# Two bursts of key-value matmuls become one behind the first denominators, and all W' units move among the queries of blocks 2 and 3

## The chip, the core and the metric

The kernel runs on one NeuronCore of one Trainium2 chip. Its engines are TensorE (PE in the profile; its weight loads are PEld), VectorE (DVE), ScalarE (ACT), GpSimd (POOL) and SyncE (SP), which here issues nearly all DMA transfers. The time is the device time of one execution in microseconds; a comparison uses the median of several executions.

## The reference

Two branches A and B of linear attention read the same x (2048 tokens, 640 features, 32 heads of 20), each with its own weights, and are mixed by a gate per token:

```
q, k, v  = x @ wqkv                       # per branch
pq, pk   = phi(q), phi(k)                 # phi(t) = where(t > 0, t + 1, exp(t)) + 1e-6
kv[h]    = pk[h]^T @ v[h]                 # 20 x 20 per head
z[h]     = sum over tokens of pk[h]
o        = (pq @ kv) / (pq . z + 1e-6)    # per head
branch   = o @ wo
out      = g * branch_A + (1 - g) * branch_B,   g = sigmoid(sum(x * gate_w))
```

## The kernel before, in words

The kernel never forms v or o. With G = pk^T x (640 by 640 per branch) the key-value product of a head is a small block of G Wv, and kv and wo are folded into one matrix W', 640 by 640 per branch: row (h, d) of W' is kv[h][d, :] times the 20 rows of wo of head h. Then branch = (pq / den) @ W'. The stages, in the order of TensorE:

1. Keys (`k_part`, `k_both`): k = x Wk by token tiles of 128; ScalarE takes the exponential, VectorE forms phi.
2. G (`g_unit`, five units per branch, k = 0 to 4): 32 matmuls of 320 columns accumulate over the 16 token tiles; ScalarE copies the result to GS, a transposing DMA puts it into GT.
3. M (`m_unit`): the blocks of kv. 55 matmuls per branch, each with 64 stationary columns in one of two column halves of the array (g = 0 or 1) and 60 or 40 moving columns, all into one PSUM bank. Units q = 0 to 4 hold six heads (120 features) each, three in each half; q = 5 holds the last two heads and uses only one half, half 0 for A and half 1 for B. VectorE then multiplies by a constant mask (L647: two instructions of 60 x 300, one of 40 x 40) and writes MB, which has six slots that A and B use in turn; slot 5 is shared, A in its upper rows and B in its lower ones.
4. W' (`wp_unit`): per unit two matmuls of 320 columns (weights MB, moving operand the rows of wo) into a pair of PSUM banks, and one eviction to WS, by VectorE for three units of A (L680), by ScalarE for the rest (L682). There are 11 units: five per branch and one joint unit for slot 5. `wp_store` writes the 600 rows to DRAM, `wp_rows` the last 40, and reads all of it back in the row order of the queries, into WPA and WPB.
5. Queries (`q_unit`): blocks b = 0 to 3 of 512 tokens, two branches, k = 0 to 4: 40 units of five matmuls of 512 columns. ScalarE takes the exponential (L743) into one of six EK slots, VectorE does min and add (L747), then max and add (L752), which releases the unit's PSUM bank.
6. Denominators (`dens`), for blocks 0 and 1 together and for blocks 2 and 3 together: 20 matmuls of 512 columns with 32 stationary columns, four of them side by side, into one bank.
7. `scale_q` per block: ScalarE adds epsilon (L787), VectorE takes the reciprocal (L793), two DMAs spread the factor over the partitions, VectorE multiplies the queries (L811).
8. Final tiles (`final`): per token tile an A half and a B half of ten matmuls, ScalarE scales A by g (L859), VectorE adds B (L865), SP stores. At most three A halves can wait for their B halves (three TS slots).

**What sets the order.** The calls at the end of the function only list operations; each gets the next priority number. `_Sched.schedule` then plans: again and again it takes the operation that can start earliest, and among those of one engine within 20 ns of the earliest the one with the lowest number (L188). It books durations by formulas (`_act_ns`, `_dve_ns`: elements / 0.96 + 68 ns for a VectorE instruction at rate 1, so 0.38 us for a mask of 300) and 180 ns between an operation and one that needs its result. The eight PSUM banks are given out in the same walk (`place`, L157 to 165): a tile of two banks takes the aligned pair that was free first, a tile of one bank the bank that was free first, or one whose pair neighbour is busy among those within 300 ns. A bank is taken again when, by the book, its last reader has ended; on the chip the new user waits on that reader's semaphore. What results is one fixed list per engine, run in that order. Reciprocals and multiplies of `scale_q` may so run earlier than their place in the list of calls.

Before, the calls stand like this: M_A between the G units of B; A's W' units between the rest; M_B behind the queries of block 0; the joint unit and B's W' units among the queries of block 1, each two queries behind (WPLAG = 2); `scale_q(0)` ahead of the queries of block 2.

Of the kernel before, what the change touches and what calls it, by code (L numbers as in the profile page):

```python
# [15 lines left out]
ACT = mybir.ActivationFunctionType  # L16
# [3 lines left out]
D = 640  # L20
H = 32
DH = 20
NT = 16
NB = 4
NC = 5
EPS = 1e-6
HALF = 320
WPLAG = 2
XW = 672
PE_GHZ = 2.4  # L30

# [255 lines left out]
def _act_ns(n, psum=True):  # L287
    return n / 1.2 + (52.0 if psum else 94.0)


def _dve_ns(n, rate=1):
    return n / (0.96 * rate) + 68.0
# [6 lines left out]
def bass_gated_mix__linear_attn_block__linear_attn_block__prompt_kernel(nc, A_x, A_wqkv, A_wo, B_x, B_wqkv, B_wo, gate_w, out):  # L299
# [6 lines left out]
    with ExitStack() as es:  # L306
        E = es.enter_context

        def sb(name, shape, dtype=dt.bfloat16):
            return E(nc.sbuf_tensor(name, shape, dtype))  # L310
# [11 lines left out]
        PQ = {X: FE[:, x, :].rearrange("p (k s) -> p k s", s=S) for x, X in enumerate(XS)}  # L322
        WP = {X: sb("WP" + X, [128, NC, D]) for X in XS}
        W5 = sb("W5", [128, D])
        MB = sb("MB", [128, 6, 120])
        WS = sb("WS", [120, 6, D])
        WD = {X: nc.dram_tensor("wrows" + X, [D, D], dt.bfloat16) for X in XS}
        GS = sb("GS", [128, NC, D])
# [48 lines left out]
        def mms(name, steps, reads, writes, cols, lat=190.0, par=1, prio=None, after=None):  # L377


            def fn(pe):  # L380
                ins = None
                for o, l, r, a, z, tp in steps():
                    ins = pe.matmul(o, l, r, start=a, stop=z, tile_position=tp, skip_group_check=True)  # L383
                return ins

            return sch.op("PE", fn, cols / PE_GHZ / par, reads=reads, writes=writes, name=name, lat=lat, prio=prio, after=after)
# [17 lines left out]
        for X in XS:  # L404
            sch.op("POOL", lambda e, X=X: e.memset(WO[X][:, :, :], 0.0), 3000, writes=[("WO", X, 0), ("WO", X, 1)], name="woz" + X)
        sch.op("POOL", lambda e: e.memset(W5[:, :], 0.0), 500, writes=[("W5", X) for X in XS], name="w5z")
        sch.op("POOL", lambda e: e.memset(MB[:, :, :], 0.0), 700, writes=[("M", q) for q in range(6)], name="mz")
        def load_x(eng, t):
            dma(eng, "xn%d" % t, XN[:, t, 0:D], xin[128 * t : 128 * t + 128, :], writes=[("XN", t)], us=0.25)

# [201 lines left out]
        def zbd(X):  # L612
            sch.op(
                "DVE",
                lambda e: e.tensor_tensor(
                    out=ZBD[X][:, :, :], in0=CB[:, C_MH : C_MH + H].unsqueeze(1).to_broadcast([128, NC, H]),
                    in1=Z32[X][:, :].unsqueeze(2).to_broadcast([128, NC, H]), op=ALU.mult,
                ),
                _dve_ns(NC * H), reads=[("Z", X, k) for k in range(NC)] + [("CB",)], writes=[("ZBD", X)], name="zbd" + X,
            )  # L620

        def m_unit(X):

            tile = _Tile(1)
            last = XS.index(X)

            def steps():
                r = []
                for q in range(6):
                    w = 12 if q < 5 else 8  # L630
                    for j in range(NC):
                        for g in (0, 1) if q < 5 else (last,):
                            at = D * j + 120 * q + 60 * g * (q < 5)
                            r.append((
                                PS[64 * g : 64 * g + 64, tile.banks[0], 60 * q : 60 * q + NC * w], WV[X][:, at : at + 64],
                                GT[X][:, j, :, 24 * q + 12 * g * (q < 5) : 24 * q + 12 * g * (q < 5) + w], j == 0, j == NC - 1, (0, 64 * g),
                            ))
                return r

            mms("m%s" % X, steps, [("GT", X, k) for k in range(NC)] + [("WV", X), ("WVP", X)], [(tile,)], 25 * 75 + 400)  # L640
            for q0, q1, g, w in ((0, 5, 0, 12), (0, 5, 1, 12), (5, 6, last, 8)):
                n = DH * (w // 4)

                def mask(e, q0=q0, q1=q1, g=g, w=w, n=n):
                    p0 = 64 * g
                    m = CB[p0 : p0 + n, C_MM : C_MM + 60].rearrange("p (k i) -> p k i", i=12)[:, :, 0:w]
                    return e.tensor_tensor(  # L647
                        out=MB[p0 : p0 + n, q0:q1, 60 * g : 60 * g + n].rearrange("p q (i k) -> p q k i", k=NC),
                        in0=PS[p0 : p0 + n, tile.banks[0], 60 * q0 : 60 * q0 + n * (q1 - q0)].rearrange("p (q k i) -> p q k i", k=NC, i=w),
                        in1=m.unsqueeze(1).to_broadcast([n, q1 - q0, NC, w]), op=ALU.mult,  # L650
                    )

                sch.op(
                    "DVE", mask, _dve_ns(n * (q1 - q0)), reads=[(tile,), ("CB",)], writes=[("M", q) for q in range(q0, q1)],
                    name="mm%s" % X,
                )

        def wp_unit(X, q):

            tile = _Tile(2)  # L660
            w = W5 if q == 5 else WO[X][:, q, :]

            def steps():
                return [
                    (PS[0:120, tile.banks[h], 0:HALF], MB[0:124, q, :], w[0:124, HALF * h : HALF * h + HALF], True, True, None)
                    for h in (0, 1)
                ]

            mms(
                "wp%s%d" % (X, q), steps, [("M", q)] + [("W5", Y) for Y in XS if q == 5] + [("WO", X, g) for g in (0, 1) if q < 5],  # L670
                [(tile,)], D + 60,
            )
            dst = WS[:, q, :].rearrange("p (h f) -> p h f", f=HALF)

            def src():
                return PS[0:120, tile.banks[0] : tile.banks[1] + 1, 0:HALF]

            name = "wpe%s%d" % (X, q)
            if X == "A" and q % 2 == 0:
                sch.op("DVE", lambda e: e.tensor_copy(dst, src()), _dve_ns(D), reads=[(tile,)], writes=[("WS", q)], name=name)  # L680
            else:
                sch.op("ACT", lambda e: e.activation(dst, src(), ACT.Copy), _act_ns(D), reads=[(tile,)], writes=[("WS", q)], name=name)  # L682

        def wp_store(X):
            dma(
                "SP", "ws" + X, WD[X].ap()[0:600, :].rearrange("(q p) f -> p q f", p=120), WS[:, 0:5, :], reads=[("WS", q) for q in range(5)],
                writes=[("WD", X, 0)], us=2.0,
            )

        def wp_rows(X):  # L690

            nat = WD[X].ap()
            p0 = 60 * XS.index(X)
            dma("SP", "ws5" + X, nat[600:D, :], WS[p0 : p0 + 40, 5, :], reads=[("WS", 5)], writes=[("WD", X, 5)], us=0.2)
            dma(
                "SP", "wp" + X, WP[X][:, :, :], nat.rearrange("(i k) f -> i k f", k=NC), reads=[("WD", X, 0), ("WD", X, 5)],
                writes=[("WP", X, k) for k in range(NC)], us=2.2,
            )
# [59 lines left out]
        def dens(b0):  # L758

            dtile = _Tile(1)  # L760

            def den():
                r = []
                for k in range(NC):
                    for x, X in enumerate(XS):
                        q = PQ[X][:, k, 512 * b0 : 512 * b0 + 1024].rearrange("p (b h f) -> p b h f", b=2, h=2)
                        for h in (0, 1):
                            g = 2 * x + h
                            r.append((
                                PS[32 * g : 32 * g + 32, dtile.banks[0], :].rearrange("p (b f) -> p b f", b=2), ZBD[X][:, k, :],  # L770
                                q[:, :, h, :], k == 0, k == NC - 1, (0, 32 * g),
                            ))
                return r

            mms(
                "den%d" % b0, den, [("ZBD", X) for X in XS] + [("PQ", X, k, b) for X in XS for k in range(NC) for b in (b0, b0 + 1)],
                [(dtile,)], 5 * 540,
            )
            return dtile

        def scale_q(b, dtile, pieces):

# [116 lines left out]
            g_unit("A", k)  # L899
        zbd("A")  # L900
        gates()
        g_unit("B", 0)
        g_unit("B", 1)
        m_unit("A")
        g_unit("B", 2)
        for q in (0, 1):
            wp_unit("A", q)
        g_unit("B", 3)
        for q in (2, 3):
            wp_unit("A", q)  # L910
        g_unit("B", 4)
        wp_unit("A", 4)
        wp_store("A")
        zbd("B")
        def queries(b):
            for X in XS:
                for k in range(NC):
                    q_unit(X, b, k)
                    q = 5 * (X == "B") + k - WPLAG
                    if b == 1 and 0 <= q < 6:  # L920
                        wp_unit("B", (q - 1) % 6)
                        if q == 0:
                            wp_rows("A")

        def finals(b):
            for t in range(4 * b, 4 * b + 4):
# [3 lines left out]
                    final(t, ((0, 320), (320, 480), (480, D)), {320: 0, D: 320})  # L930

        queries(0)
        m_unit("B")
        queries(1)
        wp_store("B")
        wp_rows("B")
        d01 = dens(0)
        scale_q(0, d01, 2)
        queries(2)
        queries(3)  # L940
        scale_q(1, d01, 2)
        d23 = dens(2)
        finals(0)
        scale_q(2, d23, 2)
        finals(1)
# [36 lines left out]
```

## Time and profile before

| | us |
|---|---|
| median of 3 executions (190.44 to 191.15) | 190.88 |
| the profiled execution | 190.88 |
| its span, first to last instruction | 189.5 |
| TensorE busy | 185.9 |
| VectorE busy | 129.8 |
| ScalarE busy | 76.5 |
| M_A, M_B: start to the next matmul | 1.06 each |
| one query unit on TensorE | 1.08 |
| first denominators, start to the next matmul | 1.19 |
| last query matmul issued, first final tile | 142.31 |
| store of B's 600 rows, reload of WPB: issue to landing | 4.9, 4.5 |

In the lines of groups, "busy us, mean ns of one, idle time just before them" stand behind the bars. In the timeline, the first two columns are start and length; the length of a merged line runs to the end of its last instruction, and matmuls overlap, so the spacing of starts tells what a stretch costs. A release named behind an arrow is the instruction that ended a wait.

### The profile page before, as it was taken

Reading aid. Unit: us, or ns where it says so; the run is one execution under the profiler, and the core shown is the slowest. Engines: PE = TensorE matmul, PEld = TensorE weight load, DVE = VectorE, ACT = ScalarE, POOL = GpSimd, SP = SyncE. Lnnn points to the kernel's source line nnn. Section 1 sums busy time; section 2 is a strip of 40 time slices with the busy share of each in tenths; the row PEclk is TensorE's granted clock in tenths of the full one; section 3 lists DMA queues with packets and bytes.
Section 4 is the critical chain, followed back from the end, with each engine's and each line's share of the span. In section 5 each row is a group of like instructions: output and inputs, shape, how many; then the busy total and the mean of one; then the engine's idle time right before and its main releaser. Section 6 shows DMA issues by size and latency. Waiting matters only on the chain.

```text
span 189.5 us, 3208 instructions
## 1 busy us (share of the span) xinstructions
PE 185.9 (98%) x1289; PEld 124.0 (65%) x1289; DVE 129.8 (68%) x275; ACT 76.5 (40%) x129; POOL 8.2 (4%) x14
## 2 busy tenths in 40 slices
PE   7999999999999999999999999999999999999995
PEld 2555555555788888888855666455556677777774
DVE  1398998999600009996179997898999959933324
ACT  2265656565311122103255478565553422332232
POOL 8900000000000000000000000000000000000000
DMA  5999699991011111112143004675000173221212
GB/s 189 298 243 177 211 388 364 337 231 33 0 35 38 35 35 38 35 35 38 35 95 102 5 22 173 166 224 170 0 0 3 44 226 92 86 89 35 73 69 69
DMA packets 31936, 21.49 MB, mean 113 GB/s; under 512 B 16818, under 2 KB 31666, under 8 KB 31922
## 3 DMA queue, kind: packets, MB, share of 16 engines
q1 hardware_dynamic: 31490, 20.80, 39.5%
q10 hardware_dynamic: 432, 0.49, 0.8%
q8 instruction: 10, 0.16, 0.4%
q14 instruction: 4, 0.03, 0.1%
HBM read 12.05 MB, written 5.31 MB: 92 GB/s over the span
## 4 chain that ended last, share of the span: by engine, by line
PE 94%; DMA 3%; SPq 1%; issue 0%; ACT 0%; DVE 0%; DVEq 0%; ACTq 0%
PE ps L383 94%; DMA WK<-in_B_wqkv_dram 3%; SPq L372 1%; ACT TS L859 0%; DVE OL L865 0%; DVEq L276 0%; ACTq L276 0%
## 5 line engine op out<-in xcount | busy, mean ns | idle before, releaser
L383 PE MATMUL ps<-WK,XT 128*128 128x512 bf16 (+2 forms) x250 | 44.0, 337 | 0.5 <-DMA WK<-in_A_wqkv_dram 0.2
L383 PE MATMUL ps<-XN,FE 128*128 128x320 bf16 x320 | 44.3, 300 | 0.0
L383 PEld LDWEIGHTS ps<-XN,FE 128*128 128x128 bf16 x320 | 37.5, 118 | 5.9
L383 PEld LDWEIGHTS ps<-WK,XT 128*128 128x128 bf16 x250 | 24.1, 98 | 20.0 <-DMA WK<-in_A_wqkv_dram 0.5
L743 ACT ACTIVATE EK<-ps 128x512 bf16<-128x512 f32 x40 | 23.9, 597 | 18.5 <-PE ps L383 16.9
L563 ACT ACTIVATE EK<-ps 128x512 bf16<-128x512 f32 (+1 forms) x42 | 21.4, 526 | 16.2 <-PE ps L383 16.2
L752 DVE SCALAR_TENSOR_TENSOR FE<-ps,EK 128x512 bf16<-128x512 f32 x40 | 26.8, 688 | 0.7
L859 ACT ACTIVATE TS<-ps,GA 128x640 f32<-128x640 f32 (+2 forms) x18 | 13.2, 734 | 29.5 <-PE ps L383 29.5
L383 PE MATMUL ps<-WPB,FE 128*128 128x320 bf16 (+1 forms) x165 | 24.7, 295 | 0.0
L383 PE MATMUL ps<-WPA,FE 128*128 128x320 bf16 (+1 forms) x165 | 24.7, 295 | 0.0
L573 DVE SCALAR_TENSOR_TENSOR FE<-ps,EK 128x512 bf16<-128x512 f32 (+1 forms) x42 | 23.9, 596 | 0.5
L865 DVE SCALAR_TENSOR_TENSOR OS<-ps,GA,TS 128x640 bf16<-128x640 f32 x15 | 13.0, 869 | 14.7 <-PE ps L383 14.7
L383 PE MATMUL ps<-XT,WQA 128*128 128x512 bf16 x100 | 22.8, 380 | 0.0
L383 PE MATMUL ps<-XT,WQB 128*128 128x512 bf16 x100 | 22.7, 379 | 0.0
L600 ACT ACTIVATE GS<-ps 128x640 bf16<-128x640 f32 x10 | 7.0, 704 | 37.0 <-PE ps L383 37.0
L383 PEld LDWEIGHTS ps<-WPA,FE 128*128 128x128 bf16 x165 | 15.9, 98 | 6.1
L383 PEld LDWEIGHTS ps<-WPB,FE 128*128 128x128 bf16 x165 | 15.8, 98 | 6.2 <-ACT TS L859 0.4
L383 PEld LDWEIGHTS ps<-XT,WQB 128*128 128x128 bf16 x100 | 11.7, 117 | 9.1
L383 PEld LDWEIGHTS ps<-XT,WQA 128*128 128x128 bf16 x100 | 11.6, 118 | 9.4 <-issue 0.4
L705 DVE SCALAR_TENSOR_TENSOR GP<-XN,GWB 128x640 bf16<-128x640 bf16 x16 | 13.3, 829 | 4.1 <-PE ps L383 3.6
L811 DVE TENSOR_TENSOR FE<-FE,RX 128x1280 bf16<-128x1280 bf16 (+1 forms) x20 | 12.6, 685 | 1.6 <-DMA RX<-factor 1.6
L567 DVE TENSOR_SCALAR EK<-EK 128x512 bf16<-128x512 bf16 (+1 forms) x42 | 11.4, 272 | 3.1
(52 smaller groups left out, 80.3 us busy)
## 6 DMA issues: line engine op xcount, KB each, us to landing
out_dram<-OS SPq DMA_DIRECT2D x15, 160.0 KB, 1.8
XN<-in_A_x_dram SPq DMA_DIRECT2D x3, 640.0 KB, 8.1
factor<-RC SPq DMA_DIRECT2D x4, 256.0 KB, 2.6
RX<-factor SPq DMA_DIRECT2D x4, 256.0 KB, 3.2
WVA<-in_A_wqkv_dram SPq DMA_DIRECT2D x1, 800.0 KB, 10.4
WQA<-in_A_wqkv_dram SPq DMA_DIRECT2D x1, 800.0 KB, 11.9
WVB<-in_B_wqkv_dram SPq DMA_DIRECT2D x1, 800.0 KB, 11.2
WQB<-in_B_wqkv_dram SPq DMA_DIRECT2D x1, 800.0 KB, 12.5
```

Of the source, the lines that this page charges most:

```text
L372: ins = e.dma_start(dst() if callable(dst) else dst, src() if callable(src) else src, transpose=transpose)
L383: ins = pe.matmul(o, l, r, start=a, stop=z, tile_position=tp, skip_group_check=True)
L563: "ACT", lambda e, ps=ps, ek=ek: e.activation(ek(), ps(), ACT.Exp), _act_ns(n), reads=[(tile,)], writes=[(es,)],
L567: "DVE", lambda e, ek=ek: e.tensor_scalar(ek(), ek(), 1.0, EPS, op0=ALU.min, op1=ALU.add), _dve_ns(n, 4),
L573: return e.scalar_tensor_tensor(out=out, in0=two(ps()), scalar=0.0, in1=two(ek()), op0=ALU.max, op1=ALU.add)
L600: "ACT", lambda e: e.activation(GS[:, k, :].rearrange("p (h f) -> p h f", f=HALF), pair(tile, HALF), ACT.Copy),
L705: lambda e, t=t: e.scalar_tensor_tensor(out=GP[:, :], in0=XN[:, t, 0:D], scalar=1.0, in1=GWB[:, :], op0=ALU.mult, op1=ALU.mult, accum_out= ...
L743: "ACT", lambda e: e.activation(ek(), PS[:, tile.banks[0], :], ACT.Exp), _act_ns(512), reads=[(tile,)],
L752: lambda e: e.scalar_tensor_tensor(out=dst, in0=PS[:, tile.banks[0], :], scalar=0.0, in1=ek(), op0=ALU.max, op1=ALU.add),
L811: return e.tensor_tensor(out=v, in0=v, in1=RX[:, xs.slot, 512 * x + w * j : 512 * x + w * j + w].unsqueeze(1).to_broadcast([128, NC, w]), ...
L859: "ACT", lambda e, acc=acc, t_ap=t_ap: e.activation(t_ap(), acc(), ACT.Copy, scale=GA[:, 0, t : t + 1]),
L865: lambda e, acc=acc, t_ap=t_ap, o_ap=o_ap: e.scalar_tensor_tensor(out=o_ap(), in0=acc(), scalar=GA[:, 1, t : t + 1], in1=t_ap(), op0=ALU.m ...
```

## The change

M of both branches is formed in one burst of 110 matmuls, ordered directly behind the first denominators (a new `after` argument); the single half-columns of unit 5 of A and of B are paired with each other. MB gets 11 slots, so that A and B no longer share any but the joint one (slot 10). Six masks follow, in the order A's two large ones, the two small ones, B's two large ones. All 11 W' units are placed among the queries of blocks 2 and 3, from the fourth query of block 2 on (WPLAG = 3), in the order A's five, the joint one, B's five; all evictions are ScalarE's; A's rows are evicted into GS, B's into WS. A's rows are stored and read back behind the sixth unit, B's behind the eleventh. `scale_q(0)` is listed behind the queries of block 2. Nothing changes in what is computed.

```diff
-WPLAG = 2
+WPLAG = 3
-        MB = sb("MB", [128, 6, 120])
+        MB = sb("MB", [128, 11, 120])
...
-        def m_unit(X):
+        def m_both(after):
+
+            tiles = [_Tile(1), _Tile(1)]
...
             def steps():
+                r = [step(x, q, g, j) for x in (0, 1) for q in range(5) for j in range(NC) for g in (0, 1)]
+                return r + [step(x, 5, x, j) for j in range(NC) for x in (0, 1)]
+
+            mms(
+                "m", steps, [("GT", X, k) for X in XS for k in range(NC)] + [("WV", X) for X in XS] + [("WVP", X) for X in XS],
+                [(t,) for t in tiles], 110 * 38 + 240, after=after,
+            )
+            for x, q0, q1, g, w in ((0, 0, 5, 0, 12), (0, 0, 5, 1, 12), (0, 5, 6, 0, 8), (1, 5, 6, 1, 8), (1, 0, 5, 0, 12), (1, 0, 5, 1, 12)):
                 n = DH * (w // 4)
+                o0 = 10 if q0 == 5 else 5 * x
...
-                    "DVE", mask, _dve_ns(n * (q1 - q0)), reads=[(tile,), ("CB",)], writes=[("M", q) for q in range(q0, q1)],
+                    "DVE", mask, _dve_ns(n * (q1 - q0)), reads=[(tiles[x],), ("CB",)], writes=[("M", q) for q in range(o0, o0 + q1 - q0)],
...
-        g_unit("B", 0)
-        g_unit("B", 1)
-        m_unit("A")
-        g_unit("B", 2)
-        for q in (0, 1):
-            wp_unit("A", q)
-        g_unit("B", 3)
-        for q in (2, 3):
-            wp_unit("A", q)
-        g_unit("B", 4)
-        wp_unit("A", 4)
-        wp_store("A")
+        for k in range(NC):
+            g_unit("B", k)
         zbd("B")
+        order = [0, 1, 2, 3, 4, 10, 5, 6, 7, 8, 9]
+
         def queries(b):
             for X in XS:
                 for k in range(NC):
                     q_unit(X, b, k)
-                    q = 5 * (X == "B") + k - WPLAG
-                    if b == 1 and 0 <= q < 6:
-                        wp_unit("B", (q - 1) % 6)
-                        if q == 0:
+                    i = 10 * (b - 2) + 5 * (X == "B") + k - WPLAG
+                    if 0 <= i < 11:
+                        wp_unit(order[i])
+                        if i == 5:
+                            wp_store("A")
                             wp_rows("A")
+                        if i == 10:
+                            wp_store("B")
+                            wp_rows("B")
...
         queries(0)
-        m_unit("B")
         queries(1)
-        wp_store("B")
-        wp_rows("B")
-        d01 = dens(0)
+        d01, den = dens(0)
+        m_both(den)
+        queries(2)
         scale_q(0, d01, 2)
-        queries(2)
         queries(3)
```

## The prediction

> **What bounds the kernel now.** I read the page's head first, then its chain of waits, then the timeline of TensorE and of VectorE around the denominators.
>
> ```profile
> span 189.5 us, 3208 instructions
> ...
> PE 185.9 (98%) x1289; PEld 124.0 (65%) x1289; DVE 129.8 (68%) x275; ACT 76.5 (40%) x129; POOL 8.2 (4%) x14
> ...
> PE ps L383 94%; DMA WK<-in_B_wqkv_dram 3%; SPq L372 1%; ACT TS L859 0%; DVE OL L865 0%; DVEq L276 0%; ACTq L276 0%
> ```
>
> The span ends with one unbroken chain of matmuls (in order of time: 177.88 us from 9.05 on). So a change counts only by the matmul time that it takes away and by the holes that it opens. The granted clock is 1.00 in every stretch.
>
> The timeline of TensorE (start, length, matmuls) shows where M and the denominators stand:
>
> ```profile
> 100.38 5.56 PE L383 MATMUL ps<-XT,WQB 128*128 128x512 bf16 x25
> 105.86 1.13 PE L383 MATMUL ps<-GTB,WVB 128*64 128x60 bf16 x55
> 106.92 3.43 PE L383 MATMUL ps<-XT,WQA 128*128 128x512 bf16 x15
> 110.19 0.44 PE L383 MATMUL ps<-W,MB 124*120 124x320 bf16 x2
> 110.47 1.24 PE L383 MATMUL ps<-XT,WQA 128*128 128x512 bf16 x5
> ...
> 122.85 2.36 PE L383 MATMUL ps<-XT,WQA 128*128 128x512 bf16 x10
> ```
>
> The reader should subtract starts. 25 query matmuls of 0.216 us take 5.40 us, but the burst M_B starts 5.48 after them: entering 64-column tiles costs 0.09. M_B itself takes 1.06; a W' unit takes 0.28.
>
> VectorE, whose work moves, on the timeline (around M_B, then behind the first denominators):
>
> ```profile
> 107.03 1.02 DVE L647 TENSOR_TENSOR MB<-ps,CB 60x300 bf16<-60x300 f32 x1
> 107.80 0.76 DVE L752 SCALAR_TENSOR_TENSOR FE<-ps,EK 128x512 bf16<-128x512 f32 x1
> 108.58 1.36 DVE L647 TENSOR_TENSOR MB<-ps,CB 60x300 bf16<-60x300 f32 x2
> 109.97 0.29 DVE L747 TENSOR_SCALAR EK<-EK 128x512 bf16<-128x512 bf16 x1
> ...
> 123.48 1.75 DVE L793 RECIPROCAL RC<-DN 128x256 bf16<-128x256 f32 x1
> 125.15 0.23 DVE L747 TENSOR_SCALAR EK<-EK 128x512 bf16<-128x512 bf16 x1
> 125.29 1.74 DVE L793 RECIPROCAL RC<-DN 128x256 bf16<-128x256 f32 x1
> 126.95 0.63 DVE L752 SCALAR_TENSOR_TENSOR FE<-ps,EK 128x512 bf16<-128x512 f32 x1
> 127.49 0.48 DVE L747 TENSOR_SCALAR EK<-EK 128x512 bf16<-128x512 bf16 x2
> ```
>
> The mask's group, with shapes kept apart (busy us, mean ns, idle before):
>
> ```profile
> L647 DVE TENSOR_TENSOR MB<-ps,CB 60x300 bf16<-60x300 f32 x4 | 4.1, 1032 | 0.1
> ```
>
> What to see: a large mask takes 1.03 us, and behind it the next instruction starts 0.77 later if it is independent, 1.07 if it is the next mask. The reciprocals start 0.73 behind the end of the denominators (123.48 against 122.85 less 0.10 for leaving their tiles) and hold VectorE 1.67 each. From there on VectorE is busy 18.73 of 19.46 us up to the last query matmul (the table by stretches, 122.85 to 142.31).
>
> **The change, part by part.**
>
> *M in one burst (TensorE).* Records inside M start in pairs, 31 ns a pair, 0.025 more for the first; five single steps take 32 ns each; leaving the tiles costs 0.085. Before: 2 x (0.09 + 1.06) = 2.30, plus 0.10 that the denominators pay to leave theirs: 2.40. After: 55 pairs with the single steps paired, 1.745, plus 0.085 to leave. No row shows 32-column tiles followed by 64-column ones; the bounds are 0 and 0.10, the six changes that the trace has cost 0.085 to 0.10, so I take 0.09. Sum 1.92: a gain of 0.48 (0.47 to 0.57).
>
> The Trainium skill ("TensorEngine Tiling (Array Packing)", Key Properties) says that changing the tiling mode drains TensorE, which the 0.09 of each row agrees with; if staying in column tiles counted as no change of mode, the gain would be 0.57, by the rule as worded 0.48.
>
> *W' units.* Still 11, 22 matmuls, 3.0 us: moved, not shortened. Three evictions go from VectorE (0.82 each) to ScalarE (0.70). With a unit's exponential (0.60) ScalarE then needs 1.20 back to back per query and W' unit (110.45 to 111.65 at the W' units of before), TensorE 1.36 (1.08 + 0.28): covered; without that cover each would cost the difference.
>
> *Memset of MB.* 697 ns grows with 1320 against 720 elements to about 1.28, at the start of POOL. The next on POOL are small memsets needed at 48.8; SP's loads of Wo, which wait on POOL, issue at 28.8. Free.
>
> *Six masks (VectorE).* They leave places with room (gate products; block 1) for the stretch that holds both reciprocals. Here lies the price. The order of each engine and the PSUM banks are fixed beforehand by the kernel's planner, which books a large mask at 0.38 us (line 654 with line 292) where the row says 1.03 (0.77 net); queries, reciprocals and W' units it books within 0.1 of their net rows. I follow its rules (lines 157 to 165, 188) only for the order. All times below are from the end of the denominators.
>
> The six masks are one chain: A's two large ones, A's small one, B's small one (both write M unit 10), B's two large ones. Between dependent ones the planner leaves 0.18 us, into which it puts whatever is ready. So VectorE's order is: reciprocal 0, mask 1, reciprocal 1, mask 2, min-add A2, mask 3, min-add A3, mask 4, max-add A2, mask 5, max-add A3, mask 6, min-add A4, min-add B0, max-add A4 (A2 is branch A, k = 2 of block 2; A0 and A1 ran before the denominators, as now). Measured rows: 0.73 + 1.67 + 0.77 + 1.67 + 1.07 + 0.32 + 0.20 + 0.30 + 0.72 + 0.77 + 0.75 + 0.77 + 0.20 + 0.20 + 0.69 = 10.8.
>
> TensorE's order: M, A2, A3, A4, B0, W'0, B1, B2, W'1, W'2. Single tiles rotate through the eight banks in pairs: (A0, A1), (denominators, M_A), (M_B, A2), (A3, A4); then B0 and B1 take the first pair, B2 A2's bank, W'0 and W'1 the second pair. W'2 needs two banks and gets those of A3 and A4, which the book thinks free 0.2 us before TensorE arrives. TensorE arrives at 1.92 + 4 x 1.08 + 0.28 + 2 x 1.08 + 0.28 = 9.0. VectorE releases A4's bank at 10.8, plus under 0.1 for the signal. A hole of 1.9. Queued behind W'2 on TensorE: everything. Bounds: 0 (another bank) to 2.2 (every booking error of the masks kept, 4 x 0.39 + 2 x 0.2, and 0.2 more for the slowed max-adds); I take 1.9, from the named bank. After it TensorE stands as late as VectorE, so it isn't paid twice: M, 18 queries and 11 W' units give TensorE 24.4 us, VectorE needs some 25 (18 x 0.80, masks 3.9, reciprocals 3.3, the first multiplies 2.96, start 0.7), and TensorE has lost 1.9.
>
> The Trainium skill ("VectorE: DVE Perf Modes", the table of cycles in the errata section) gives 120 + 300 cycles at 0.96 GHz for such an instruction from PSUM, 0.44 us; the row of 1.03 contradicts it. By the page the masks would be late by some 0.3 in all, the hole would shrink to 0.3, and the time would be near 191.0.
>
> *Path of WP.* Behind the tenth W' unit come: eviction ends 1.18 after the matmuls (110.47 to 111.65), store 4.95 (issue 118.39, next step 123.36), reload 4.5. W'10 (fourth query of block 3, 10 W' units before it) ends at 1.92 + 12 x 1.08 + 11 x 0.28 = 18.0, so WP_B lands at 28.6. The last query ends at 24.4; the A halves of two output tiles (2 x 1.36) and the second denominators (1.2) fill until 28.3. Missing: 0.3, both being late alike through the hole. Bounds 0 (a third A half is put first) to 1.0. WP_A, five units earlier, lands some 5 us before it is needed. On SP nothing stands behind these transfers: the factors of blocks 0 and 1 are then under way already.
>
> *Scaling of blocks 0 and 1.* Moved behind the queries of block 2: its multiplies (4 x 0.74) fill gaps and end long before 24.4.
>
> Sum: -0.48 + 1.9 + 0.3 = +1.7. The profiled run's own time is 190.88 (span 189.5, 1.4 around it), which is also the median: 192.6.
>
> **The rivals.**
> 1. *No hole* (not slower): the bank of W'2 is one that is free, the mask's lateness disappears in the rotation. For it: M_B's lateness (its masks net 1.2 over the book) opened no hole in block 1, TensorE idle 0.0 there. Against: one M, no reciprocals, fewer banks taken. 190.88 - 0.48 = 190.4. It decides if W'2's banks are free before 9.0, that is if VectorE's list is shorter by 1.9.
> 2. *Half a hole*: a query goes ahead of W'2, the lateness is met later against banks with 0.5 to 1.5 of room: 0.3 to 1.2, giving 190.7 to 191.9.
> 3. *W' units slip*: if pairs of banks are rare, the last W' comes two queries later (2 x 1.36), WP_B too, one more A half covers 1.36: 1.4 on top, 194.0.
>
> **How the numbers follow.** Hole as computed (1.2 to 2.2): 0.6, 191.5 to 193.6 with the bounds of the other terms; rival 1: 0.17; rival 2: 0.18; rival 3: 0.05. I forecast 192.6. Covering all but rival 3 and the edges: 190.3 to 193.1. About 0.5% (0.95 us) is what can be told from no change. Slower than 191.83: nine tenths and more of the first case, a little of rival 2, rival 3: 0.62. Faster than 189.93: no mechanism reaches it, 0.02. Same: 0.36.
>
> **What would show it.** M as one group of 110 matmuls behind the denominators, 1.7 to 1.9 long; TensorE's first hole since the start, near 2 us, in front of the third W' unit, ended by a max-add (L752's line); six masks of unchanged length; behind the second denominators a wait on WPB of under 1 us. Wrong, if TensorE runs without holes up to the final tiles, or if the hole stands elsewhere and is ended by a DMA.

## The result and the profile after

The changed kernel takes 196.38 us (median of 6 executions, 195.07 to 197.73) where the kernel before took 190.91 beside it (6 executions, 190.44 to 191.47). The ratio is 1.0281, with a 95% interval from 1.0227 to 1.0336. It is slower, as forecast, but by 5.5 us instead of 1.7, and 196.38 lies far above the range's upper end of 193.1.

The six times fall into two groups: 195.07 to 195.81 in three executions, where the granted clock is 1.000 on average, and 196.95 to 197.73 in the other three, where it is 0.991. The profiled one, 196.96 (span 195.6, again 1.4 around it), is of the second group.

The head of the page, and its chain:

```profile
span 195.6 us, 3206 instructions
...
PE 188.0 (96%) x1289; PEld 124.7 (64%) x1289; DVE 129.4 (66%) x272; ACT 78.3 (40%) x132; POOL 8.7 (4%) x14
...
PE ps L383 81%; DMA wrowsB<-WS 4%; DMA WK<-in_B_wqkv_dram 3%; DVE MB L649 2%; DMA WPB<-wrowsB 2%; DVE RC L799 2%; DVE FE L758 1%; SPq L372 1%; DVE EK L753 1%; ACT EK L749 1%; ACT WS L683 0%; ACT TS L865 0%; DVE OL L871 0%; ACTq L276 0%; DVEq L276 0%
```

Matmuls carried 94% of the chain before and carry 81% now. Two stretches of other work have come into it, and the same chain in order of time (start, length, engine, tile, line) shows which:

```profile
126.26 1.01 DVE MB L649
127.28 0.51 DVE EK L753 x2
127.81 0.70 DVE FE L758
...
128.56 8.89 PE ps L383 x46
...
138.07 0.60 ACT WS L683
...
138.71 7.58 DMA wrowsB<-WS
...
146.35 4.24 DMA WPB<-wrowsB
...
150.73 42.28 PE ps L383 x305
```

First VectorE, whose list is shown here from the last mask to a max-add (L758, the old L752), holds TensorE until 128.56. Then, from 138.07 on, the last eviction, B's store of 7.58 us and B's reload of 4.24 end only at 150.73. From there to the last tile the matmuls run on without a stop.

TensorE on the timeline (start, length, matmuls, in brackets the wait and what ended it):

```profile
117.26 0.98 PE L383 MATMUL ps<-GTA,WVA 128*64 128x60 bf16 x50
118.07 0.96 PE L383 MATMUL ps<-GTB,WVB 128*64 128x60 bf16 x50
...
119.11 3.43 PE L383 MATMUL ps<-XT,WQA 128*128 128x512 bf16 x15
122.38 1.24 PE L383 MATMUL ps<-XT,WQB 128*128 128x512 bf16 x5
123.79 0.45 PE L383 MATMUL ps<-WOA,MB 124*120 124x320 bf16 x2 [0.16 <-DVE MB L649]
...
128.56 0.48 PE L383 MATMUL ps<-WOA,MB 124*120 124x320 bf16 x2 [1.88 <-DVE FE L758]
...
150.73 4.43 PE L383 MATMUL ps<-WPB,FE 128*128 128x320 bf16 x20 [2.43 <-DMA WPB<-wrowsB]
154.94 1.69 PE L383 MATMUL ps<-WPA,FE 128*128 128x320 bf16 x10
```

The burst stands where it was announced. The wait before 123.79 is in front of the first W' unit (five matmuls of 0.216 behind 122.38 end at 123.46: 0.33 lost), the one before 128.56 in front of the third. The 20 matmuls from 150.73 to 154.94 take 4.21 us; the 20 of WPA just before them need 2.8. The table by stretches says why (stretch, length, busy time and instructions of PE, PEld, DVE, ACT, POOL, granted clock, DMA share, GB/s):

```profile
147.00:150.73 3.73, 1.30 (x22) 0.48 (x22) 1.75 (x1) 1.74 (x3) 0.00 (x0) 1.00 0.66 222
150.73:154.94 4.21, 4.21 (x20) 2.54 (x21) 0.88 (x1) 0.00 (x0) 0.00 (x0) 0.64 0.35 105
```

After the second hole the granted clock is 0.64 on average for 4.2 us.

Two transfers on the way to WPA and WPB run together. SP's issues, and the page's list of DMA issues (KB, us to landing):

```profile
138.32 0.35 SPq L372 DMA_DIRECT2D WPA<-wrowsA  x1
138.71 0.43 SPq L372 DMA_DIRECT2D wrowsB<-WS  x1
146.35 0.35 SPq L372 DMA_DIRECT2D WPB<-wrowsB  x1
```

```profile
WPA<-wrowsA SPq DMA_DIRECT2D x1, 800.0 KB, 5.8
...
wrowsB<-WS SPq DMA_DIRECT2D x1, 750.0 KB, 7.6
```

A's reload and B's store start 0.4 us apart. Before, they stood 5.1 us apart, so that the reload had landed when the store was issued, and the same two rows read 4.3 and 4.9:

```profile
113.28 0.36 SPq L372 DMA_DIRECT2D WPA<-wrowsA  x1
118.39 0.34 SPq L372 DMA_DIRECT2D wrowsB<-WS  x1
```

```profile
WPA<-wrowsA SPq DMA_DIRECT2D x1, 800.0 KB, 4.3
...
wrowsB<-WS SPq DMA_DIRECT2D x1, 750.0 KB, 4.9
```

**Where 6.1 us of span (195.6 less 189.5) come from**, each subtracted from the timelines:

| | us | forecast |
|---|---|---|
| M and its tile changes: 1.94 against 2.40 | -0.46 | -0.48 |
| wait in front of the first W' unit | +0.33 | 0 |
| hole in front of the third W' unit | +2.05 | +1.9 |
| wait for WPA | +0.2 | 0 |
| hole in front of the first use of WPB | +2.5 | +0.3 |
| low clock behind it: 1.5 in 20 matmuls, 0.2 in the next ones | +1.7 | no term |
| start-up, shorter in this execution | -0.2 | |
| sum | +6.1 | +1.7 |

Without the low clock the sum is +4.4, and the executions with full clock are 4.2 to 4.9 above the median of before.

### The profile page after: what moved, and what is told of

The parts are those of the page before. It is cut to its first block, busy times and chain, and to the rows that moved or that the text cites. A ratio compares the mean times of both kernels' runs of the same rounds, so it can differ in the third digit from the quotient of the medians.

```text
span 195.6 us, 3206 instructions
## 1 busy us (share of the span) xinstructions
PE 188.0 (96%) x1289; PEld 124.7 (64%) x1289; DVE 129.4 (66%) x272; ACT 78.3 (40%) x132; POOL 8.7 (4%) x14
## 4 chain that ended last, share of the span: by engine, by line
PE 81%; DMA 9%; DVE 6%; SPq 1%; ACT 1%; issue 1%; ACTq 0%; DVEq 0%
PE ps L383 81%; DMA wrowsB<-WS 4%; DMA WK<-in_B_wqkv_dram 3%; DVE MB L649 2%; DMA WPB<-wrowsB 2%; DVE RC L799 2%; DVE FE L758 1%; SPq L372 1%; DVE EK L753 1%; ACT EK L749 1%; ACT WS L683 0%; ACT TS L865 0%; DVE OL L871 0%; ACTq L276 0%; DVEq L276 0%
## 5 line engine op out<-in xcount | busy, mean ns | idle before, releaser
L383 PE MATMUL ps<-XN,FE 128*128 128x320 bf16 x320 | 43.8, 300 | 0.0
L383 PE MATMUL ps<-WPB,FE 128*128 128x320 bf16 (+1 forms) x165 | 26.1, 307 | 2.4 <-DMA WPB<-wrowsB 2.4
L758 DVE SCALAR_TENSOR_TENSOR FE<-ps,EK 128x512 bf16<-128x512 f32 x40 | 27.4, 691 | 0.9
L865 ACT ACTIVATE TS<-ps,GA 128x640 f32<-128x640 f32 (+2 forms) x18 | 13.2, 735 | 33.9 <-PE ps L383 33.9
L383 PEld LDWEIGHTS ps<-WPB,FE 128*128 128x128 bf16 x165 | 16.4, 101 | 9.5 <-issue 2.9
L711 DVE SCALAR_TENSOR_TENSOR GP<-XN,GWB 128x640 bf16<-128x640 bf16 x16 | 13.2, 825 | 4.2 <-PE ps L383 3.6
L567 DVE TENSOR_SCALAR EK<-EK 128x512 bf16<-128x512 bf16 (+1 forms) x42 | 11.3, 270 | 2.8
## 6 DMA issues: line engine op xcount, KB each, us to landing
WVB<-in_B_wqkv_dram SPq DMA_DIRECT2D x1, 800.0 KB, 11.2
```

The source lines that it names most:

```text
L567: "DVE", lambda e, ek=ek: e.tensor_scalar(ek(), ek(), 1.0, EPS, op0=ALU.min, op1=ALU.add), _dve_ns(n, 4),
L711: lambda e, t=t: e.scalar_tensor_tensor(out=GP[:, :], in0=XN[:, t, 0:D], scalar=1.0, in1=GWB[:, :], op0=ALU.mult, op1=ALU.mult, accum_out= ...
L758: lambda e: e.scalar_tensor_tensor(out=dst, in0=PS[:, tile.banks[0], :], scalar=0.0, in1=ek(), op0=ALU.max, op1=ALU.add),
L865: "ACT", lambda e, acc=acc, t_ap=t_ap: e.activation(t_ap(), acc(), ACT.Copy, scale=GA[:, 0, t : t + 1]),
```

## The experiments

The theory with which I went in: two separate costs, the masks on VectorE (2.05 and 0.33) and the store of B slowed by A's reload (2.5, and the clock behind it). The rivals: that booking or moving the burst cannot help because VectorE simply has too much to do there, that B's path is late for another reason (its length, not the company it has), and that the burst's 0.46 is not a gain at all. Times are medians beside the kernel before on the same chip.

### 1. The masks booked as measured (e1_book)

```diff
-"DVE", mask, _dve_ns(n * (q1 - q0)), reads=[(tiles[x],), ("CB",)], ...
+"DVE", mask, 1000 if n * (q1 - q0) == 300 else 270, reads=[(tiles[x],), ("CB",)], ...
```

> The changed kernel, with the planner booking a large mask at 1.00 us and a small one at 0.27 (as measured) in place of 0.38 and 0.11; nothing else is edited, so only the planner's order and banks move. Theory 1 (the hole of 2.05 us in front of the third W' unit is the difference between booked and real masks, met at one PSUM bank): the hole falls to 0.4 or less, the 0.35 in front of the first W' unit too; the wait for WPB stays at 2 to 3 us, with the low clock behind it. Time 193.5 to 194.5. Rival (VectorE is overloaded behind the denominators whatever the planner knows): holes of about 2 us stand elsewhere, 195.5 to 197.

Measured: 194.74 us (194.38 to 196.93), ratio 1.0221 (1.0172 to 1.0270); before 190.90. A little above what the theory gave. The hole of 2.05 in front of the third W' unit is gone. Smaller ones stand in its place: 0.3 in two parts around the second W' unit, 0.4 between the fourth and the fifth, and 0.9 in front of the third of three W' units in a row, this one ended by ScalarE's eviction. Together they are 1.7, against 2.4. The hole in front of WPB stays, and in this profiled execution the clock behind it stays full (timeline of TensorE, then the table by stretches):

```profile
149.85 2.88 PE L383 MATMUL ps<-WPB,FE 128*128 128x320 bf16 x20 [2.48 <-DMA WPB<-wrowsB]
```

```profile
149.70:154.00 4.30, 4.15 (x31) 3.03 (x32) 2.16 (x4) 0.00 (x0) 0.00 (x0) 1.00 0.34 103
```

So 20 matmuls cost 2.72 here and 4.21 in the profile above, behind holes of nearly equal length. The book is part of the first cost, not the whole of it: a right book buys 0.7 us of holes.

### 2. Without A's store and reload (e2_noA)

A's W' units are computed, but not stored; WPA is filled early with the plain rows of A's Wo, so the A half of the output is another one.

```diff
+            if X == "A":
+                dma("SP", "wpA", WP["A"][:, :, :], wo["A"].rearrange("(i k) f -> i k f", k=NC), ...)
...
-                        if i == 5:
-                            wp_store("A")
-                            wp_rows("A")
```

> The changed kernel without the store and the reload of A's rows: WPA is filled early with plain rows of A's Wo (so A's half of the output leaves W' out); A's W' units and their evictions still run. Theory 1 (B's store took 7.6 us in place of 4.9 because A's reload shares the DMA engines with it, and the low clock follows from the hole that this made): B's store takes 4.9 to 5.3 us, the wait for WPB is 0.3 or less, the clock is 1.00 throughout; the hole of 2.0 in front of the third W' unit stays. Time 190.9 - 0.5 + 2.4 + 0.2 = 193.0. Rival (the W' units simply come too late, contention or not): the wait for WPB stays above 2 us, the low clock too, 195.5 to 197.

Measured: 193.46 us (193.31 to 193.81), ratio 1.0133 (1.0116 to 1.0149). B's store, alone now, takes what it took before, and the hole shrinks to a rest (DMA issues, then the timeline):

```profile
wrowsB<-WS SPq DMA_DIRECT2D x1, 750.0 KB, 4.9
```

```profile
148.45 2.88 PE L383 MATMUL ps<-WPB,FE 128*128 128x320 bf16 x20 [0.32 <-DMA WPB<-wrowsB]
```

The clock is full in all four executions. The hole in front of the third W' unit is untouched, 2.03. This tells the company from the length: the same eviction, store and reload, without A's transfers beside them, miss their time by 0.3 to 0.4, as forecast, and not by 2.5.

### 3. Both together (e4_book_noA)

The edits of 1 and 2, WPA filled as in 2.

> Both edits: masks booked as measured, and no store and reload of A's rows (WPA holds plain rows of A's Wo, A's half leaves W' out). Theory 1: no hole above 0.4 us remains, and what is left is the single burst's gain of 0.48: 190.4 to 191.0. Rivals: one of the two holes stays, 192.5 or more; or the gain of the burst is not there, 190.9 or more without any hole.

Measured: 192.56 us (192.50 to 192.83), ratio 1.0085 (1.0071 to 1.0098). Missed by 1.6. The hole in front of WPB is gone, but the small holes of experiment 1 (0.3, 0.4 and 0.95, together 1.7) remain. The two costs add up: from experiment 2 to this one 0.9 is recovered (193.46 to 192.56), about the 0.7 of the booking and the 0.3 that was left in front of WPB. The burst's gain shows in the sum: 1.7 of holes less 0.46 make 1.2, and the span is 190.8 against the 189.5 of before. In both kernels without A's transfers the time is 1.7 above the span instead of 1.4, which is 0.3 of the miss; why, no run shows.

### 4. Masks of two units instead of five (e7_short)

The same program, order and bookings; only the four large masks handle 120 of their 300 columns, so that three units of each half of MB stay zero and the output is another one.

```diff
-                def mask(e, x=x, q0=q0, q1=q1, o0=o0, g=g, w=w, n=n):
+                def mask(e, x=x, q0=q0, q1=min(q1, q0 + 2) if q0 == 0 else q1, o0=o0, g=g, w=w, n=n):
```

> The changed kernel with the four large masks on two of their five units only (60 x 120 in place of 60 x 300; the other units' blocks of M are left out, so W' is not complete), booked by the planner as before: the order on all engines and the banks are those of the changed kernel, only the masks are shorter, about 0.5 us each between the rows of 0.28 (40 elements) and 1.03 (300). Theory 1 (the hole in front of the third W' unit is the masks' real length over the booked one): 4 x 0.5 less lateness, the hole of 2.05 falls to 0.2 or less and the 0.35 in front of the first W' unit goes; the wait for WPB stays at 2 to 2.6. Time 192.5 to 194. Rival (reciprocals and queries on VectorE make it, not the masks): 1.5 or more of the hole stays, 194.5 to 196.

Measured: 194.31 us (193.01 to 195.34), ratio 1.0185 (1.0140 to 1.0229). The mask's group, and TensorE around the first W' units:

```profile
L649 DVE TENSOR_TENSOR MB<-ps,CB 60x120 bf16<-60x120 f32 x4 | 2.0, 488 | 0.0
```

```profile
124.02 0.44 PE L383 MATMUL ps<-WOA,MB 124*120 124x320 bf16 x2
...
126.45 1.05 PE L383 MATMUL ps<-WOA,MB 124*120 124x320 bf16 x4
```

With masks of 0.49 us instead of 1.01 the wait in front of the first W' unit is gone, and the second and third W' units form one group, with 0.3 lost inside it instead of 2.05. The hole in front of WPB stays (2.6). So the length of the masks, with the order unchanged, made all of the first wait and 1.7 of the second. At full clock this kernel takes 193.01 and 193.86, the changed one 195.07 to 195.81: about 2 us, as the two holes had.

### 5. The burst behind the queries of block 0 (e3_early)

```diff
         queries(0)
+        m_both(None)
         queries(1)
         d01, den = dens(0)
-        m_both(den)
-        queries(2)
         scale_q(0, d01, 2)
+        queries(2)
...
-                    i = 10 * (b - 2) + 5 * (X == "B") + k - WPLAG
+                    i = 10 * (b - 1) + 5 * (X == "B") + k - WPLAG
```

> The changed kernel with the burst behind the queries of block 0 and the W' units among the queries of blocks 1 and 2, reciprocals as before; the booking is as in the changed kernel. Theory 1: the masks are again late by some 2 us against the book, but no reciprocal stands between them, so the hole in front of a W' unit is 0 to 1; WPA and WPB come 10 us before they are needed; the burst alone gains 0.38 (it does not share the denominators' tile change). Time 190.5 to 191.5. Rival (lateness of the masks alone makes the hole, wherever they stand): a hole of 1.5 to 2, 192 to 192.6.

Measured: 192.80 us (192.73 to 193.31), ratio 1.0103 (1.0083 to 1.0124). It is 3.6 below the changed kernel, but the cost does not vanish as expected: 1.05 is lost in front of the second W' unit (ended by the max-add, as in the changed kernel), and 1.2 in all at the first final tiles, where VectorE is late after waiting 2.3 us at one place for the factor of `scale_q`. Less the burst's gain, these are the 1.9 by which it is slower than before.

### 6. The same with the masks booked as measured (e5_early_book)

> The burst behind the queries of block 0 with W' among blocks 1 and 2, and the masks booked as measured. Theory 1: the hole of 1.05 in front of the second W' unit goes, the ones at the first final tiles (1.2 in all) may stay, since VectorE and the factors' transfers are as late there: 191.5 to 192.0. Rival (VectorE has no room for the masks): holes of 1 or more elsewhere in blocks 1 and 2, 192.5 or more.

Measured: 192.26 us (191.44 to 192.90), ratio 1.0068 (1.0048 to 1.0088). The holes at the first W' units are at most 0.1 now: here, where no reciprocals stand between the masks, the book is the whole of the matter. What is left is one hole of 1.3 in front of the second denominators, again ended by a max-add, with VectorE's wait of 2.3 us for the factor ahead of it. The rest of the profiled execution's time (192.90) is start-up, which no edit touches: its first matmul of G starts at 49.88, against 48.82 before.

### 7. The burst between the two branches of block 0 (e6_mid)

The W' units move half a block further ahead, and the masks are booked as measured.

```diff
+                if (X, b) == ("B", 0):
+                    m_both(None)
...
-                    i = 10 * (b - 2) + 5 * (X == "B") + k - WPLAG
+                    i = 10 * b + 5 * (X == "B") + k - 5 - WPLAG
...
         d01, den = dens(0)
-        m_both(den)
-        queries(2)
         scale_q(0, d01, 2)
+        queries(2)
```

> The burst between the two branches' queries of block 0, W' units from there to the middle of block 1, reciprocals as before, masks booked as measured: all masks, W' units, stores and reloads are over before the denominators. Theory 1: no hole above 0.3, the reload of A and the store of B may overlap at no cost, the single burst gains 0.38: 190.4 to 190.8. Rival (the masks do not fit beside queries anywhere): holes of 1 or more, 191.5 or more.

Measured: 193.00 us (192.54 to 193.90), ratio 1.0117 (1.0095 to 1.0138). Missed: worse than experiment 6. Two holes, 1.37 at the last B queries and 1.06 at the first final tiles, and ahead of them VectorE's longest wait (timeline of VectorE, then of SP):

```profile
133.54 3.03 DVE L817 TENSOR_TENSOR FE<-FE,RX 128x1280 bf16<-128x1280 bf16 x4 [3.41 <-DMA RX<-factor]
```

```profile
118.82 0.34 SPq L372 DMA_DIRECT2D wrowsB<-WS  x1
124.94 0.35 SPq L372 DMA_DIRECT2D WPB<-wrowsB  x1
125.34 1.59 SPq L372 DMA_DIRECT2D factor<-RC  x2
130.51 1.12 SPq L372 DMA_DIRECT2D RX<-factor  x2
```

SP runs its list in order. WPB's reload waits for B's store until 124.94, and the writes of the factor, which stand behind it, issue only at 125.34, their reads at 130.51. VectorE's multiplies wait for them, and the queries' min and max behind the multiplies wait too, so PSUM banks come free late. This was the point at which I formed a second theory: where the transfers of W' stand ahead of the factor on SP, it is the order on SP that costs.

The order is only the smaller part of it. From the start of the first reciprocal to the issue of the first write it is 2.5 us here and 1.8 in experiment 9, where no reload stands ahead: 0.7. From that write to the first read it is 5.2 us here, with WPB's reload in flight (issued at 124.94, landed 4.8 later), and 2.7 there: 2.5. So the larger part is once more a transfer slowed by its company.

### 8. The kernel before, with A's reload beside B's store (e8_overlap)

Nothing of the change, only A's reload held back until B's last eviction.

```diff
-reads=[("WD", X, 0), ("WD", X, 5)],
+reads=[("WD", X, 0), ("WD", X, 5)] + [("WS", 4)] * (X == "A"),
...
-                        if q == 0:
-                            wp_rows("A")
...
+        wp_rows("A")
         wp_store("B")
```

> The kernel before, with the reload of WPA held back until the last eviction of B's W' units, so that it is issued beside B's store as in the changed kernel. Theory 1 (store and reload slow each other): B's store takes 7 to 8 us in place of 4.9, A's reload 5.5 to 6 in place of 4.3; WPA and WPB still land 10 us before they are needed, so the time is 190.9 within 0.5. Rival (the store was slow for another reason, its place or what the core did beside it): 4.9 to 5.2.

Measured: 193.15 us in one execution, 2.3 above the 190.81 of before. The transfers did what the theory said (DMA issues):

```profile
WPA<-wrowsA SPq DMA_DIRECT2D x1, 800.0 KB, 5.8
...
wrowsB<-WS SPq DMA_DIRECT2D x1, 750.0 KB, 8.8
```

8.8 and 5.8 instead of 4.9 and 4.3, in a kernel that has none of the change. But the time, expected to stay, rose, for the reasons of experiment 7: B's longer store moves WPB's reload on SP to 127.51 and the factor's writes behind it to 127.91 (125.26 before), these take 5.3 us to the first read at 133.21 (3.4 before), and the multiplies of block 0 wait:

```profile
136.14 3.03 DVE L811 TENSOR_TENSOR FE<-FE,RX 128x1280 bf16<-128x1280 bf16 x4 [3.56 <-DMA RX<-factor]
```

They start at 131.44 in the kernel before. TensorE then has two holes, 1.4 in front of the third B query of block 3 and 0.8 in front of the second half tile, both ended by a max-add: 2.2 of the 2.3 of this one execution.

### 9. Both reloads behind the factor (e9_late)

Experiment 7, with the two reloads taken out of `wp_rows` into a function of their own, which is called behind `scale_q(0)` and reads the multiplied queries' mark, so that no reload can pass the factor.

```diff
+        def wp_load(X):
+            nat = WD[X].ap()
             dma(
                 "SP", "wp" + X, WP[X][:, :, :], nat.rearrange("(i k) f -> i k f", k=NC),
-                reads=[("WD", X, 0), ("WD", X, 5)], ...
+                reads=[("WD", X, 0), ("WD", X, 5), ("PQS", "A", 0)], ...
...
         scale_q(0, d01, 2)
+        wp_load("A")
+        wp_load("B")
         queries(2)
```

> The kernel of the run e6_mid (burst inside block 0, masks booked as measured) with both reloads of W' held back behind the first scaling multiplies, so that the factors of blocks 0 and 1 pass SP and the DMA engines first. Theory 1 (the holes of 1.4 and 1.1 us there come from the factor of block 0, which waited behind the stores and reloads; VectorE stood 3.4 us in front of its multiplies): VectorE's wait for the factor falls to 1 us or less, the two holes go, WPA and WPB land by 139, before the first final tile: 190.4 to 190.8, the burst's 0.38 shows. Rival (VectorE has no room, factor or not): holes of 1 us and more stay, 192 or more.

Measured: 190.62 us (190.41 to 191.14, 12 executions) beside 190.93 (23 executions), ratio 0.9989 (0.9975 to 1.0003). SP's order and VectorE's multiplies now:

```profile
125.54 2.31 SPq L372 DMA_DIRECT2D factor<-RC  x2
128.20 2.15 SPq L372 DMA_DIRECT2D RX<-factor  x2
132.12 0.34 SPq L372 DMA_DIRECT2D WPA<-wrowsA  x1
132.56 0.38 SPq L372 DMA_DIRECT2D WPB<-wrowsB  x1
```

```profile
131.20 3.03 DVE L820 TENSOR_TENSOR FE<-FE,RX 128x1280 bf16<-128x1280 bf16 x4
```

VectorE's wait for the factor in front of these multiplies falls from 3.41 to 0.1 (the max-add ahead of them ends at 131.06), B's store has 4.9 again, TensorE has no hole among the queries and final tiles. 2.4 us are back, with the same burst, masks and W' units as experiment 7. The medians differ from before by 0.31; the single burst saves about 0.36 at such a place, where it does not share the denominators' tile change (1.94 against 2.30). The interval just reaches 1, so beside the kernel before this version is not shown to be faster.

The two reloads now overlap: WPA's takes 4.4 and WPB's 5.8, 6.2 from the first issue to the last landing. Apart they took 4.3 and 4.5 before.

### 10. The kernel before with late reloads (e10_before_late)

The same `wp_load`, in the kernel before.

> The kernel before, with both reloads held back in the same way; the control for e9_late. Theory 1: VectorE's wait for the factor (0.67 us) shrinks, TensorE has no hole before or after, so the time is 190.9 within 0.2, and a difference between e9_late and this run is the burst's own. Rival (late reloads cost by themselves): a wait for WPA or WPB at the first final tiles, 191.5 or more.

Measured: 190.96 us (190.59 to 191.31, 12 executions), ratio 1.0003 (0.9989 to 1.0017). Late reloads alone gain nothing where the transfers were not in each other's way. What experiment 9 has over experiment 7 is thus a repair of the moved transfers, no gain of its own. As the control it also isolates the burst: the medians of experiments 9 and 10 differ by 0.34, the means by 0.31, with a 95% interval from 0.12 to 0.49 worked out from the 12 times of each. That is the size of the 0.36.

## Why the prediction was wrong, point by point

**What bounds the kernel.** Right: every term that moved the time is a change of matmul time or a hole of TensorE, and they add up to the span. One sentence was read too far: that the granted clock is 1.00 in every stretch holds for a TensorE without holes, and the forecast was of one with holes.

**M in one burst.** Right to 0.02: 0.46 against 0.48. The change from 32-column tiles to those of 64 columns, which had no row, costs the 0.09 that was taken (0.31 from the last denominator matmul to the burst, less 0.216).

**W' units.** Right: 0.28 each, ScalarE covers its evictions in the changed kernel. The planner put two of B's units in one gap, so that it was four queries, not five, from the sixth to the eleventh.

**Masks.** The mechanism, the place and the releasing instruction were right, and VectorE ran exactly the order worked out. The size, 1.9 against 2.05, was right partly by luck. VectorE's list on the timeline:

```profile
117.89 1.75 DVE L799 RECIPROCAL RC<-DN 128x256 bf16<-128x256 f32 x1
...
123.38 0.26 DVE L649 TENSOR_TENSOR MB<-ps,CB 40x40 bf16<-40x40 f32 x1
123.50 0.27 DVE L753 TENSOR_SCALAR EK<-EK 128x512 bf16<-128x512 bf16 x1
123.78 0.29 DVE L649 TENSOR_TENSOR MB<-ps,CB 40x40 bf16<-40x40 f32 x1
...
126.26 1.01 DVE L649 TENSOR_TENSOR MB<-ps,CB 60x300 bf16<-60x300 f32 x1
127.28 0.49 DVE L753 TENSOR_SCALAR EK<-EK 128x512 bf16<-128x512 bf16 x2
127.81 1.29 DVE L758 SCALAR_TENSOR_TENSOR FE<-ps,EK 128x512 bf16<-128x512 f32 x2
```

The denominators end at 117.17, so A4's bank is released (128.51) at 11.3 and not at 10.8: the sum of steps has no term for the second small mask (0.32 from 123.78 to the next start), and the last mask holds its successor for 1.02, not 0.77. Against that, TensorE came 0.35 later than 9.0, because the first W' unit had waited: it goes on at 123.79, 0.15 behind the end of A's small mask (123.64), the last reader of M_A's bank, which it takes by the order of banks in the forecast. That wait stood in the forecast's own list: the small mask was to start at 6.23 and TensorE to arrive at 6.24, and a mask that starts as TensorE arrives is a wait. Only the third W' unit was compared. Experiment 4 shows that both holes hang on the masks' length, and experiment 1 that the wrong book is worth only 0.7 of the 2.4 there: what the true lengths leave is a stretch with six masks and two reciprocals in it. Which part of the remaining 1.7 is VectorE's load and which the place where the planner puts W' units in a row stays open.

**Path of WP.** This is the step that failed, in the sentence that took B's store at 4.95 from its row and in the one that said WP_A "lands some 5 us before it is needed". The row of 4.95 is of a store with no other large transfer of W' beside it. In the changed kernel the same steps give, from the end of the last W' unit (137.55): eviction 1.1 (1.18 forecast), store to the next issue 7.7 (4.95), reload 4.4 with what leads to the matmul (4.5): 13.2 instead of 10.6. The 2.55 more is the hole of 2.5, which experiment 2 takes away by taking away A's transfers and nothing else on B's path, and experiment 8 makes the slower transfers in the kernel before. The "5 us" of WP_A was not worked out at all. By the forecast's own rows the sixth W' unit ends at 11.2, WP_A lands at 21.8, and its first use comes at 24.4: 2.6 early. Of these the planner's pairing took 1.1, the store's way 0.3, and the reload, itself slowed by B's store, 1.3; WPA landed 0.2 too late. And that the two paths meet could be read from the forecast's own rows: by them A's reload runs from 17.3 to 21.8 and B's store from 19.2 to 24.1 behind the denominators. In the changed kernel A's path takes 12.2 us from the end of its last W' unit to the landing (131.86 to 144.1), and B's begins 5.7 behind it (137.55).

The Trainium skill ("DMA: Bandwidth & Descriptors", Rules for kernel authors) says of two transfers to disjoint partition halves that both are spread over the same 16 engines and so serialize. For a reload beside a store the rows agree in the main: one after the other the two would take 4.3 + 4.9 = 9.2 us, together they took 8.0 in the changed kernel (138.32 to 146.3) and 9.2 in experiment 8 (118.22 to 127.4). For two reloads they do not: 4.3 + 4.5 = 8.8 apart, 6.2 together in experiment 9.

**On SP.** "On SP nothing stands behind these transfers" was right for the changed kernel, where the factors are out of the way. In experiments 7 and 8, where WPB's reload is issued just ahead of the factor, what stands behind it decides the time, by its place on SP and by the company in flight.

**The granted clock.** The forecast had no term for it. In the profiled execution it cost 1.7, behind the longest hole. It is the main reason why six executions spread over 2.7 us: the medians of the two groups, 195.21 and 196.96, lie 1.75 apart.

**Scaling, memset.** Right: no wait on them in the chain.

**Rivals.** Rival 1 (no hole) and rival 2 (half a hole) fell, by the wait that the profile shows. Rival 3 named the right object, a WP_B that comes late, with the wrong cause: no W' unit came two queries later than planned. None of the rivals let two transfers meet. The range's upper end was made from bounds of 0 to 1.0 on the path of WP, and those bounds came from which half tile is put first, not from the durations: the store's own row got no bound at all. The recorded 193.1 also lies below the 193.6 that the working gives as the upper edge of its main case.

## What to carry to other kernels

A transfer's row is the price of that transfer in the company it had: before a store and a reload are moved, write down when each is in flight, and where two of them meet, take the sum of both as the upper bound of each, and follow what a later landing does to the transfers behind it. When a list of one engine is worked out to find a hole, compare every user of its results with it, not only the one that looks worst. And a term for a hole of some 2.5 us on TensorE should hold the clock behind it.

## What the runs showed of the hardware

- Behind a hole of about 2.5 us on TensorE the granted clock was 0.64 over the next 4.2 us in the profiled execution of the changed kernel; behind an equal hole (2.48) in experiment 1 it stayed at 1.00. Over all executions with that hole the mean clock was 0.991 in 6 of 14 (3 of 6 of the changed kernel, 1 of 4 in experiment 1, 2 of 4 in experiment 4), and in none of those of the kernels without it. That the hole and the low stretch lie at the same place in the executions without a profile is inferred. Behind the hole of 2.05 in the same profile the clock stayed at 1.00.
- The Trainium skill ("TensorE: Matmul & The Clock Gate", Why this matters for your kernels) advises against idle gaps above some 3 us, and Part 1 of that page describes a free-running window. That a free-running window catches some holes and not others fits the 6 of 14, but no run here shows the window; the gap in front of the low clock was shorter here, about 2.5 us.
- A store of 750 KB and a reload of 800 KB issued 0.4 us apart take 7.4 to 8.8 and 5.7 to 5.9 us (the changed kernel and experiments 1, 4 and 8), against 4.9 and 4.3 apart. Two reloads issued 0.4 us apart take 4.4 and 5.8 (experiment 9).
- The factor's writes, 256 KB each, take 2.7 us from the first issue to the first read where no reload is in flight (experiments 9 and 10), 3.4 where WPB's reload was issued 1.9 us ahead (the kernel before), and 5.2 to 5.3 where it was issued 0.4 ahead (experiments 7 and 8).
- The mask's time goes with its columns less than in proportion: 1.01 us for 60 x 300, 0.49 for 60 x 120, 0.26 to 0.29 for 40 x 40.
